# Running sums of pair units from products of two tokens' alphas, one mask operation for both score banks, and a new order

## The chip, the cores and the metric

The kernel runs on one core of one Trainium2 chip. Its metric is the device time of one execution in microseconds: 162.4 us is the median of three runs (162.36 to 163.71). A time in the text below that has a start and an end is counted from the first instruction of the profiled execution.

Five engines take part. TensorE multiplies matrices and writes PSUM, which has eight banks. VectorE, ScalarE and GpSimd work element by element[...]. SyncE (SP) issues the loads and stores, and ScalarE's queue issues a few DMA transposes. The profile calls them PE (and PEld for its weight loads), DVE, ACT, POOL and SP.

## What is computed

For 4 batches and 8 heads, 768 tokens and 48 columns a head, a gated linear recurrence runs over the tokens, and its result goes through a low-rank mixing over the tokens and a two-layer MLP:

```python
for t in range(S):
    state = alpha[:, :, t, :, None] * state + einsum('bhd,bhe->bhde', k[:, :, t], v[:, :, t])
    y[:, :, t] = einsum('bhd,bhde->bhe', q[:, :, t], state)
# x: y with the heads side by side, [4, 768, 384]
h = x.transpose(0, 2, 1) @ U @ V            # U is 768 x 32, V is 32 x 768
u = x + h.transpose(0, 2, 1)
out = u + maximum(u @ w_ch1, 0) @ w_ch2     # 384 -> 1536 -> 384
```

All inputs and the output are fp32; the matmuls run on bf16 operands.

## The kernel before

**Chunks.** The recurrence is computed in chunks. Inside a chunk, the logarithms of the alphas are summed up along the tokens by a matmul with a triangle of ones; the exponentials of the sums (`aa`) and of their negatives (`ai`) scale q and k (`rq`, `rk`); the scaled q and k are transposed (`qT`, `kT`), multiplied to scores, masked to the causal half (`pm`), and multiplied with v (`rv`). A state `st` carries the chunk's end to the next one. Its factor `tot` comes from the sums over the whole chunk.

**Two kinds of units.** Each batch has six units, u0 to u5. In batches 2 and 3 (`stage_gla`) a unit is 128 tokens of all eight heads. In batches 0 and 1 (`PAIR`, function `stage_pair`) a unit is 256 tokens of four heads: a partition holds two neighbouring tokens, 64 partitions make one chunk of 128 tokens, and a unit has two chunks one above the other. So a pair unit's `lt`, the logarithms, has two halves of 192 columns, for the first (j = 0) and the second (j = 1) token of each pair. The running sum up to the first token of a pair is the sum of all pairs before it and its own first token; up to the second token it is the sum of all pairs up to it. In the old form the sum is made of three matmuls: the triangle `upto` with the first half, written to both halves of the output (384 columns), `below` (without the pair itself) with the second half onto the first 192 columns, and `upto` with the second half onto the other 192. Four small matmuls with `onesel` make the totals, two for each half.

**Scores.** The score matmul of every unit writes two PSUM banks of 128x512, one for the even and one for the odd heads. A VectorE operation for each bank multiplies it with the mask, `maskp` in a pair unit (L542) and `maskc` in the others (L769), and writes half of `pm` in bf16.

**Mixing and MLP.** After its six units a batch goes through the mixing (`stage_mix`, to `uT`, the transposed input of the MLP), then `mlp1` (24 groups of three matmuls of 384 columns at L953, a group named here by half of the tokens and by its 128 rows of w1, each followed by a relu on ScalarE or VectorE, L963 and L965), then `mlp2` (L983, 18 groups of four or five matmuls, an addition on VectorE at L995, a store). For batch 3, `rq` and `rk` are transposed by DMA (issued on ScalarE's queue, L734), for the other batches by TensorE.

**The order.** Every step is put in a list by `P.add` with the engines that it may run on, what it reads and what it writes. The string `TABLE` is the order in which the steps are issued: a number is the step's place in the list, and a letter after it its engine where there is a choice (A ScalarE, V VectorE, G GpSimd). It was found by a search over a cost model, the class `Plan`. Each engine takes its steps in the order of the table. The costs and latencies in `P.add` and `Plan` decide only which buffer or PSUM bank of several a step is given and how many filler matmuls run before 28 us on idle TensorE; they hold nothing back on the chip. A step waits on the chip for the steps that it depends on, and for buffers that come free. `port=True` marks steps that share a port of VectorE and GpSimd.

**Loads.** Every load is one DMA of 192 KB on SP's queue into one of 36 buffers, in the order of the table; the weights come through the same buffers and are cast to bf16. SP's loads and stores and the DMA transposes share the same DMA engines.

Of the kernel before, what the change touches and what calls it, by code (L numbers as in the profile page):

```python
# [159 lines left out]
75 2 3 4 5 209 211 67 76 163 165 79 234 214 167 69 77 68 170V 212 215G 236 217 172 238 213 216V 166 169V 218 171 174V 220V 173V 175 176 83 70 81 237  # L160
168 219A 71 78 164G 80 178 221 179 223 73 72 87 74 0 241G 180 222 181 84 186 259 239 188 210G 240G 190 189 261 224 225 226 177 264 263 192V 1 193G 187G
242 227 243 244A 262 245V 229 230 231 194 246 232V 282 191 196A 233V 228 247 248 182 195 284 197A 184A 201 198 183 85 287 285 265G 82 88 202 266V 267
203 269A 235G 89 268 199 204 200 86 270A 185A 286 249 250 251 271 90 91 7 288G 254 289V 8 260G 95 6 33 99 252 256 35 31 23 39 10 290 258A 253 272 273
292A 19 41 21 37 27 25 107 29 291 255 205 274 275 293A 276 294 257A 295 296 283A 277 57 297 298 279 206 9G 410 34G 32G 412 278 299 208A 207V 300 301
302 304V 101 92 100 47 96 97 94 415 280A 281A 303A 13 16 305 306 93 43 55 45 49 14A 311 308 314 317 307A 51 63 59 53 456 315 309 433 98 103 312 17V
313A 458 318 320 310V 323 321 324 322V 325V 435 11 20V 319V 36A 316A 340 338 342 362 339V 61 436 461 438 341A 366 22G 42G 364 24A 460 363A 12A 38V 40V
365V 352 328 437 367A 414 30A 459 65 102 111 108 104 109 105 329V 343V 26V 28V 463V 106 462G 326 348 349A 506 413 330 368 354 360 355V 331V 336 508
353V 416V 439V 112 346 332 511 347A 369A 333A 372 373V 334 335V 337V 327V 440G 358 356 465 344 464 467V 510 361A 509 359A 442 411G 417G 115 113 444V
345A 357A 466A 418 441 350 419 425 443V 420V 421V 351A 46A 48A 468 15 44G 56G 50G 110 114 426 469 445 422 370 116 424 423 446 470 371A 52A 380 386 54G
64G 429 430 432V 447 58A 431A 434A 374 375 448 452 62G 427 428V 449 60V 66V 450 387 381 453 454A 117 481 483 376 457V 455V 476 471 477 382 486 485 529  # L170
484 531 377 472 512G 514 388 473V 487V 513V 474 516V 515 392 489 488V 451G 383 532 533 517A 491V 479V 389 482G 490 478 492A 480A 535G 534 653 393 496
497 493 518 498G 536G 495 494 119 394 655 537 398 538 379 378 123 390 127 399 499 520 395 519 475G 500G 530G 507A 539A 656 659V 501 521 544 540A 658
657 541 660G 503 661 545 400 502 662A 505A 522 504A 663 542 543 524 547 523G 546V 664V 526 672 549 551A 548 525 550A 674 118 391 124 121 120 129 131
528V 135 133 122 125 527V 665 552 404 676 677 553A 675 692 712 554 654G 401 666 137 139 667 132 126 564 559 555 560 556 561 405 406 557 670 562 668 565
566 694 714 567 563V 669 558A 587 585 589 696 716 695 715 717 590A 732 671V 679V 568V 573 609 605 407 610V 698G 579 615 606V 616V 571 580A 586A 588A
752 591 734 592A 697 700 577 678V 572V 701V 754 673G 719G 699G 756 737 755 680 607 134 613 608V 578V 595 575 682 687 574V 681V 688 614V 611 576A 736
612A 596A 603 702 581 601 703V 689G 597 569 599 604A 582A 735 598A 570A 863 600A 602A 683V 128 385 136 384 408 758G 739G 693G 738G 704 684 705 685 686
583 707 617 740 722 584A 708 723V 718G 865 618 690 867 130 141 403 706 159 151 147 138 757G 709V 691V 866 741A 713G 619 710 761 762A 720 742 593 759
760A 594A 721V 629 620 143 409 146 396 621 622 402 868 727 743V 630 728 140 148 145 155 724 744 898 952 916 753A 733G 18 870G 729G 763 711V 765 726 764
635 636 745 725 746 631 623 747 637 900 901 624 730 750 748 749V 766 767V 632 880 731A 882 902 751A 883 903 885 884 872 625 869G 638 626 768 628 871  # L180
641 642 152 153 627 149 397 142 769V 780 775 776 770 777 771 781 782 643 918 919 772 887G 904G 647 954 648 778 783 649 773 889 920 779V 784V 144 634
150 811 922G 923G 934 956 955 812A 921 924 774V 829 813 873 787 830V 814V 160 874 799 800V 875 650 819 793 815 794V 644 816V 936 809 827 825 810V 823
791 828V 785 905G 881G 864G 886G 899G 788A 925 907 876 906 888 957G 824V 826V 786V 877 797 803 893 821 878 157 792A 798A 938 894 804V 156 154 161 805
806V 801 158 941V 802V 937 879A 939 822A 820A 817 926 890 908 940G 818A 928 959 789 790A 892 891 909 917G 895G 958G 853 910 795 796V 943 942 807 808V
896 831 911 912 833 854 935G 960 914 947 929 927 913V 930 931V 948 949V 915A 832A 858 834 835 859 633 162 855 953V 836 837 944 946 961 945 860 838 839
950 932 652 963 962 646 964 651 645 856 843 840 861 951V 933A 965A 897A 966 848 967A 841 978 968 973 980 975 974 979 844 849 970 969 845 976 977A 857
842 862 981 850 971 982V 1015 1016V 1025 1007 1011 1013 1027 972V 991 1008V 993 994A 1028A 1026A 851 846 1009 995 1001 999 1023 1002A 1014A 1024A 992A
1021 1019 1029 1022V 1012V 1017 1010A 1020A 1018A 983 1046 1047 1030V 1048 1049 984A 989 990V 987 1051 1005 1003 1004V 639 1050 985 1052 997 1053 986V
988V 1054 640 1055 852 996A 1031 1041 1036 998V 1042 1006A 1000A 1043 1044 1032 1037 1038 1033 1056 1045 847 1039 1040 1034 1057 1059 1060 1035 1058
1061  # L190
# [8 lines left out]
def kernel(  # L199
# [37 lines left out]
    QUAD = ()  # L237
    TRD = {(3, c): "kq" for c in range(NC)}
# [78 lines left out]
    pms = Pool(slots("pm", 3, [C, HP, 2, C], BF16))  # L317
# [13 lines left out]
    P.warm = lambda: nc.tensor.matmul(ps[:, 7, :], lhsT=filler[:, 0:128], rhs=filler, start=True, stop=True)  # L331

# [96 lines left out]
    def stage_pair(b, u, sprev, xb):  # L429
# [10 lines left out]
        lt = Buf(lts)  # L440
        P.add({"ACT": 435}, lambda e: nc.scalar.activation(jh(lt()[:, :, 0:D]), raw(at), AF.Ln), r=[at], w=[lt])  # L441
# [17 lines left out]
        def f_cum(e):  # L459
            l2 = jh(lt()[:, :, 0:D])  # L460
            nc.tensor.matmul(cb()[:, 0:DM].rearrange("p (i h d) -> p i h d", i=2, d=D), lhsT=upto, rhs=l2[:, 0:1].to_broadcast([C, 2, HP, D]), start=True, stop=False)
            nc.tensor.matmul(cb()[:, 0:Q], lhsT=below, rhs=l2[:, 1], start=False, stop=False)
            nc.tensor.matmul(cb()[:, Q : 2 * Q], lhsT=upto, rhs=l2[:, 1], start=False, stop=False)
            nb = 2 if b == 0 else 1
            if b == 0:
                nc.tensor.matmul(cb()[:, DM : DM + 8], lhsT=ident, rhs=offd.rearrange("p a b -> p (a b)"), start=False, stop=False)
            tot4 = cb()[:, DM : DM + 4 * nb].rearrange("p (c a b) -> p c a b", c=2, a=2)
            for a in range(2):
                for j in range(2):
                    nc.tensor.matmul(  # L470
                        tot4[:, :, a, :], lhsT=lt()[:, HP * j + 2 * a : HP * j + 2 * a + 2, :].rearrange("t h w -> t (h w)"),
                        rhs=onesel[:, :, 0:nb], start=False, stop=(a == 1 and j == 1),
                    )

        P.add({"PE": mm(DM, Q, Q, 4, 4, 4, 4, *([8] if b == 0 else []))}, f_cum, r=[lt], w=[cb])
# [48 lines left out]
        def f_sc(e):  # L524
            for n in range(4):
                a, j = n // 2, n % 2
                for par in range(2):
                    o = 64 * par
                    for c in range(2):
                        r = slice(64 * c, 64 * c + 64)  # L530
                        nc.tensor.matmul(  # L531
                            sc[par]()[r, n * C : (n + 1) * C],
# [6 lines left out]
        def f_mask(par):  # L539
            s2 = sc[par]().rearrange("p (a j c) -> p a j c", a=2, j=2)  # L540
            dst = pm()[:, :, par, :].rearrange("p (a j) c -> p a j c", j=2)
            nc.vector.tensor_tensor(dst, s2, maskp.to_broadcast([C, 2, 2, C]), op=ALU.mult)  # L542

        for par in range(2):
            P.add({"DVE": 605}, lambda e, par=par: f_mask(par), r=[sc[par]], w=[(pm, par)])
# [63 lines left out]
        if apart:  # L609
            yb = [Buf(bank) for _ in range(2)]  # L610
            def f_yn(e):
                for h in range(HP):
                    for j in range(2):
                        for c in range(2):
                            r = slice(64 * c, 64 * c + 64)
                            for m in parts:
                                nc.tensor.matmul(
                                    yb[c]()[m, h * D : (h + 1) * D], lhsT=pm()[r, (h // 2) * 2 + j, h % 2, m], rhs=raw(rv)[r, j, h, :],
# [3 lines left out]
            P.add({"PE": mm(*[D] * 8)}, f_yn, r=[(rv, 0), (rv, 1), (pm, 0), (pm, 1)], w=[(yb[0], 0), (yb[1], 0)], mode=tile)  # L622
# [22 lines left out]
        def f_y(e):  # L645
# [12 lines left out]
            for h in range(HP):  # L658
                for j in range(2):
                    nc.tensor.matmul(  # L660
                        y[:, :, h, :], lhsT=pm()[:, (h // 2) * 2 + j, h % 2, :], rhs=rv()[:, j, h, :, :],
                        start=False, stop=(h == HP - 1 and j == 1), skip_group_check=True,
                    )
# [400 lines left out]
```

## Time and profile before

| | us |
|---|---|
| median of three runs | 162.4 |
| the profiled execution's own time | 164.51 |
| its span, first to last instruction | 162.7 |
| TensorE busy | 153.9 |
| VectorE busy | 119.3 |
| ScalarE busy | 85.4 |
| GpSimd busy | 52.8 |
| first MLP matmul starts at | 28.06 |
| first MLP matmul of batch 2 starts at | 101.67 |
| last addition of VectorE starts at | 159.79 |

A row of a timeline reads: start, length, engine, line, operation, what it writes and reads, shape, count; in brackets the idle time of the engine before it, and what ended that. A row of a table by stretches reads: from and to, length, and for each of PE, PEld, DVE, ACT and POOL the busy time with the number of instructions; then TensorE's granted clock, the busy share of the DMA engines and GB/s. In the page's slices each digit is a tenth of busy time in one fortieth of the span. Matmuls overlap: one of 384 columns is listed with 320 ns and more, but they follow each other every 0.16 us. The DMA engines are busy for nearly the whole time up to 120 us.

### The profile page before, as it was taken

What the parts mean: (1) busy time and instruction counts of PE and PEld (TensorE: products, weight loads), DVE (VectorE), ACT (ScalarE), POOL (GpSimd) and SP (SyncE); (2) the same over time, 40 slices, a digit from 0 to 9 for tenths busy, and PEclk for the clock granted to TensorE, in tenths of its full rate; (3) what the DMA queues carried; (4) which work ended last, traced back from release to release, by engine and by line L of the source; (5) the groups of instructions that cost most, each with busy time, mean ns of one, the idle gap of its engine ahead of it and who ended that gap; (6) DMA issues with size and microseconds to landing.
All of it is one profiled execution on the core that took longest, in us unless ns stands there. A gap on an engine that the chain in (4) does not pass through costs nothing.

```text
span 162.7 us, 4734 instructions
## 1 busy us (share of the span) xinstructions
PE 153.9 (95%) x1821; PEld 99.6 (61%) x1821; DVE 119.3 (73%) x275; ACT 85.4 (52%) x224; POOL 52.8 (32%) x85
## 2 busy tenths in 40 slices
PE   6899999999999999999999999896899999999992
PEld 2457677566666665766676657463576747666662
DVE  6289995788997999977487969696698777234441
ACT  5748788958836678676954661601701311472000
POOL 5256741217336460215975005533370000000000
PEclk9999999999999999999999999999999999999999
DMA  5999999998999967979988879999994631002223
GB/s 128 288 299 272 270 234 290 286 310 254 297 320 258 241 144 162 194 155 213 201 194 162 201 141 210 192 156 180 223 246 15 186 106 28 0 0 76 97 109 133
DMA packets 89910, 30.39 MB, mean 187 GB/s; under 512 B 83584, under 2 KB 89856, under 8 KB 89888
## 3 DMA queue, kind: packets, MB, share of 16 engines
q1 hardware_dynamic: 83360, 28.52, 73.9%
q10 hardware_dynamic: 6528, 1.57, 6.7%
q8 instruction: 14, 0.23, 0.6%
q14 instruction: 8, 0.07, 0.1%
HBM read 23.79 MB, written 4.72 MB: 175 GB/s over the span
## 4 chain that ended last, share of the span: by engine, by line
PE 67%; SPq 15%; DMA 12%; issue 2%; ACT 1%; DVE 1%; POOL 0%; ACTq 0%; DVEq 0%; POOLq 0%
PE ps L983 27%; PE ps L953 23%; SPq L411 10%; DMA io<-in_moe_w_ch_dram 4%; DMA io<-in_v_dram 4%; DMA qt<-rq 3%; DMA io<-in_q_dram 2%; PE ps L759 2%; PE ps L507 2%; PE ps L743 2%; SPq L387 2%; SPq L1009 2%; PE ps L926 1%; PE ps L851 1%; PE ps L531 1%
## 5 line engine op out<-in xcount | busy, mean ns | idle before, releaser
L983 PE MATMUL ps<-w_sb,h1t 128*128 128x384 bf16 (+2 forms) x300 | 53.5, 320 | 0.0
L953 PE MATMUL ps<-uT,w_sb 128*128 128x384 bf16 x288 | 51.0, 326 | 1.3 <-ACT h1t L963 0.9
L953 PEld LDWEIGHTS <-w_sb 128*128 128x128 bf16 x288 | 27.1, 98 | 17.8 <-issue 1.5
L983 PEld LDWEIGHTS <-h1t 128*128 128x128 bf16 x300 | 26.7, 98 | 16.0 <-issue 1.8
L963 ACT ACTIVATE h1t<-ps 128x384 bf16<-128x384 f32 x52 | 23.6, 497 | 20.7 <-PE ps L953 12.7
L965 DVE TENSOR_SCALAR h1t<-ps 128x384 bf16<-128x384 f32 x44 | 22.7, 552 | 11.1 <-PE ps L953 11.0
L769 DVE TENSOR_TENSOR pm<-ps,maskc 128x512 bf16<-128x512 f32 x24 | 15.1, 683 | 3.3 <-PE ps L759 3.3
L995 DVE TENSOR_TENSOR ou<-ub,ps 128x384 f32<-128x384 bf16 (+2 forms) x19 | 9.9, 528 | 9.2 <-PE ps L983 7.8
L542 DVE TENSOR_TENSOR pm<-ps,maskp 128x512 bf16<-128x512 f32 x24 | 15.6, 683 | 0.5 <-PE ps L531 0.5
L722 POOL TENSOR_TENSOR rk<-io,ai 128x384 bf16<-128x384 f32 x10 | 9.2, 923 | 19.1 <-DMA io<-in_k_dram 13.9
L342 POOL CAST rv<-io 128x384 bf16<-128x384 f32 x18 | 9.4, 527 | 16.5 <-DMA io<-in_v_dram 16.1
L338 ACT CAST xb<-ps 128x192 bf16<-128x192 f32 (+1 forms) x22 | 7.7, 377 | 12.7 <-PE ps L851 6.1
L492 POOL TENSOR_TENSOR rk<-io,ai 128x384 bf16<-128x384 f32 x7 | 6.8, 965 | 11.6 <-DMA io<-in_k_dram 7.3
L722 POOL TENSOR_TENSOR rq<-io,aa 128x384 bf16<-128x384 f32 x10 | 9.1, 914 | 4.2 <-DMA io<-in_q_dram 3.1
L911 DVE TENSOR_TENSOR ub<-xb,ps 128x384 bf16<-128x384 bf16 x18 | 8.6, 549 | 1.8 <-PE ps L903 1.8
L695 ACT ACTIVATE ai<-ps 128x384 bf16<-128x384 f32 x12 | 5.8, 498 | 4.9 <-PE ps L685 3.5
L441 ACT ACTIVATE lt<-io 128x384 bf16<-128x384 f32 x12 | 6.1, 524 | 3.6 <-DMA io<-in_alpha_dram 3.6
L342 POOL CAST w_sb<-io 128x384 bf16<-128x384 f32 x10 | 4.9, 509 | 9.4 <-DMA io<-in_moe_w_ch_dram 9.4
L696 ACT ACTIVATE aa<-ps 128x384 bf16<-128x384 f32 x12 | 5.8, 496 | 3.6 <-POOL rk L722 2.1
L338 ACT COPY kt<-ps 128x512 bf16<-128x512 bf16 x10 | 5.9, 587 | 3.0 <-PE ps L743 1.3
L492 DVE TENSOR_TENSOR rq<-io,aa 128x384 bf16<-128x384 f32 x7 | 4.5, 649 | 3.9 <-ACT aa L478 3.3
L676 ACT ACTIVATE lt<-io 128x384 bf16<-128x384 f32 x12 | 6.1, 522 | 2.0 <-DMA io<-in_alpha_dram 2.0
(133 smaller groups left out, 242.8 us busy)
## 6 DMA issues: line engine op xcount, KB each, us to landing
io<-in_alpha_dram SPq DMA_DIRECT2D x24, 192.0 KB, 4.1
io<-in_k_dram SPq DMA_DIRECT2D x24, 192.0 KB, 4.1
io<-in_q_dram SPq DMA_DIRECT2D x24, 192.0 KB, 4.2
io<-in_v_dram SPq DMA_DIRECT2D x24, 192.0 KB, 4.1
io<-in_moe_w_ch_dram SPq DMA_DIRECT2D x24, 192.0 KB, 4.1
out_dram<-ou SPq DMA_DIRECT2D x24, 96.0 KB, 3.2
out_dram<-ou SPq DMA_DIRECT2D x11, 192.0 KB, 1.9
out_dram<-ou SPq DMA_DIRECT2D x1, 128.0 KB, 1.7
```

Source lines behind the costliest of these rows:

```text
L338: nc.scalar.copy(dst, src)
L342: nc.gpsimd.tensor_copy(dst, src)
L411: lambda e: nc.sync.dma_start(t().rearrange("p (h j) d -> p h (j d)", j=2), src[b, hs, sl, :].rearrange("h (p j) d -> p h (j d)", j=2)),
L492: eng.tensor_tensor(jh(dst()[:, :, 0:D]), raw(a), jh(x()), op=ALU.mult)
L542: nc.vector.tensor_tensor(dst, s2, maskp.to_broadcast([C, 2, 2, C]), op=ALU.mult)
L722: eng.tensor_tensor(dst()[:, :, 0:D], a(), x(), op=ALU.mult)
L769: nc.vector.tensor_tensor(pm()[:, :, par, :], s2, maskc.to_broadcast([C, HP, C]), op=ALU.mult)
L953: nc.tensor.matmul(hb()[:, 0:TW], lhsT=w1_sb[:, ct, jt * 128 : (jt + 1) * 128], rhs=uT()[:, ct, tt * TW : (tt + 1) * TW], start=(ct == 0), ...
L963: nc.scalar.activation(dst, hb()[:, 0:TW], AF.Relu)
L965: nc.vector.tensor_scalar_max(dst, hb()[:, 0:TW], 0.0)
L983: nc.tensor.matmul(hb()[:, 0 : hi - lo], lhsT=h1()[:, jt, c * C : (c + 1) * C], rhs=w2_sb[:, jt, lo:hi], start=(jt == 0), stop=(jt == NJ - ...
L995: nc.vector.tensor_tensor(ou()[:, lo:hi], base()[:, c, lo:hi], hb()[:, 0 : hi - lo], op=ALU.add)
```

## The change

Four things differ.

1. In a pair unit a new step multiplies the second token's alphas by the first's, in place in the load buffer, in fp32, 128x192, on VectorE or GpSimd. The logarithm, taken after it, then holds the first token's value in its first half and the pair's sum in its second. The running sums become three matmuls of 192 columns each (`below` with the pairs, the identity with the first tokens, `upto` with the pairs), and two small matmuls make the totals.
2. One VectorE operation masks both score banks, over a view of the two PSUM banks, 128x1024 elements. `pm` is laid out with the parity ahead of the head, and its readers follow.
3. The stores of the pair batches may cover part of a row. They cover the whole row as before, since only batch 3 splits its last output.
4. The table is new. It has 1050 steps in place of 1062: 24 masks are gone and 12 products are there.

The core of the diff, without the table and without the other readers of `pm`:

```diff
+    PROD = (0, 1)
...
-    pms = Pool(slots("pm", 3, [C, HP, 2, C], BF16))
+    pms = Pool(slots("pm", 3, [C, 2, HP, C], BF16))
...
+    def two(x):
+        i, j = sorted(t.idx for t in x)
+        return ps[:, i : j + 1 : j - i, :]
+
+    def one(x, par):
+        return ps[:, sorted(t.idx for t in x)[par], :]
...
+        prod = b in PROD
+
+        def f_prod(e):
+            eng = nc.gpsimd if e == "POOL" else nc.vector
+            eng.tensor_tensor(raw(at)[:, 1], raw(at)[:, 0], raw(at)[:, 1], op=ALU.mult)
+
+        if prod:
+            P.add({"DVE": 240, "POOL": 470}, f_prod, r=[at], w=[at], port=True)
         P.add({"ACT": 435}, lambda e: nc.scalar.activation(jh(lt()[:, :, 0:D]), raw(at), AF.Ln), r=[at], w=[lt])
...
+            if prod:
+                nc.tensor.matmul(cb()[:, 0:Q], lhsT=below, rhs=l2[:, 1], start=True, stop=False)
+                nc.tensor.matmul(cb()[:, 0:Q], lhsT=ident, rhs=l2[:, 0], start=False, stop=False)
+                nc.tensor.matmul(cb()[:, Q : 2 * Q], lhsT=upto, rhs=l2[:, 1], start=False, stop=False)
+            else:
+                nc.tensor.matmul(cb()[:, 0:DM].rearrange("p (i h d) -> p i h d", i=2, d=D), lhsT=upto, rhs=l2[:, 0:1].to_broadcast([C, 2, HP, D]), start=True, stop=False)
+                nc.tensor.matmul(cb()[:, 0:Q], lhsT=below, rhs=l2[:, 1], start=False, stop=False)
+                nc.tensor.matmul(cb()[:, Q : 2 * Q], lhsT=upto, rhs=l2[:, 1], start=False, stop=False)
...
-                for j in range(2):
+                for j in range(1 if prod else 0, 2):
...
-        def f_mask(par):
-            s2 = sc[par]().rearrange("p (a j c) -> p a j c", a=2, j=2)
-            dst = pm()[:, :, par, :].rearrange("p (a j) c -> p a j c", j=2)
-            nc.vector.tensor_tensor(dst, s2, maskp.to_broadcast([C, 2, 2, C]), op=ALU.mult)
-
-        for par in range(2):
-            P.add({"DVE": 605}, lambda e, par=par: f_mask(par), r=[sc[par]], w=[(pm, par)])
+        def f_mask(e):
+            s2 = two(sc).rearrange("p r (a x) -> p r a x", a=2)
+            m2 = maskp.rearrange("p o j c -> p o (j c)").unsqueeze(1).to_broadcast([C, 2, 2, 2 * C])
+            nc.vector.tensor_tensor(pm().rearrange("p r (a j) c -> p r a (j c)", j=2), s2, m2, op=ALU.mult)
+
+        P.add({"DVE": 1140}, f_mask, r=[sc[0], sc[1]], w=[pm])
...
-        for par in range(2):
-            P.add({"DVE": 605}, lambda e, par=par: f_mask(par), r=[sc[par], "maskc"], w=[(pm, par)])
+        def f_mask(e):
+            s2 = two(sc).rearrange("p r (hp c) -> p r hp c", c=C)
+            nc.vector.tensor_tensor(pm(), s2, maskc.unsqueeze(1).to_broadcast([C, 2, HP, C]), op=ALU.mult)
+
+        P.add({"DVE": 1140}, f_mask, r=[sc[0], sc[1], "maskc"], w=[pm])
```

What the two tables say of the steps that the text below uses, with the numbers turned into names (b1u2 is unit 2 of batch 1; cum the running sums; m1 a group of the first MLP layer, by half and rows; rv, d, sc, y the cast of v, the state's matmul, the scores and the output; X the DMA transposes; w1.g a cast of w1's quarter g):

```
products, new: VectorE  b0u4 b0u0 b0u1 b0u3 b0u5 b1u0 b1u3, GpSimd  b0u2 b1u1 b1u2 b1u4 b1u5
SP, old:   b0u2.a b0u0.a ... (16th) b0u5.a ... (24th) b0u5.v ... (30th) w1.2 b1u2.a w1.2 w1.2 (33rd)
SP, new:   b0u0.a b0u2.a b0u4.a ... (19th) b0u5.a ... (26th) b0u4.v ... (30th) w1.1 w1.0 w1.0 w1.0 (33rd) ... (45th) w1.2
TensorE, old, before the MLP:  b1u2.cum ... b1u1.cum, m1 0.7 ...   new:  b1u1.cum, m1 0.0 ...
VectorE, old:  uT00 uT11 uT12 w1.0 uT10 relu ...
VectorE, new:  uT00 uT10 w1.1 relu w1.1 w1.3 relu b1u0.rq b1u3.product w1.2 relu relu relu ...
SP, batch 3, old:  ... b3u0.k u2.k u1.q u4.a [store] u3.k u3.q [store] u2.q [store] u0.v u1.k [store] u2.v u5.k u4.q u4.k u3.v ...
SP, batch 3, new:  ... b3u0.q u0.k u0.v u1.a u1.q [store] u3.q u2.k u3.k [store] u1.k u1.v u5.q u2.q u4.a u5.k u3.v ...
GpSimd, batch 3, old:  u0.rq ... u0.rk u1.rq u2.rk u3.rk u3.rq u2.rq u1.rv u0.rv u1.rk u2.rv ...
GpSimd, batch 3, new:  u0.rk [one copy for the mixing] u3.rq u0.rv u2.rk u1.rq u1.rv u1.rk u3.rk u2.rq u5.rk u3.rv ...
ScalarE, new:  b3u0.Xq ... u0.Xk ... u3.Xq relu relu u1.Xq relu u1.Xk u5.ai u3.Xk relu u4.ln u2.Xk u2.Xq relu ...
TensorE, MLP of batch 2, old:  three m1, b3u0.sc, five m1, u4.cum, six m1, u0.d, two m1, u1.d, ...
TensorE, MLP of batch 2, new:  two m1, b3u0.d, five m1, u0.sc, two m1, u1.d, three m1, u0.y, ...
```

## The prediction

> **What bounds the kernel now.** I read the page's busy time and its 40 slices first, then the busy time by stretch, then TensorE's timeline at the two places where the stretches have holes.
>
> ```profile
> span 162.7 us, 4734 instructions
> ...
> PE 153.9 (95%) x1821; PEld 99.6 (61%) x1821; DVE 119.3 (73%) x275; ACT 85.4 (52%) x224; POOL 52.8 (32%) x85
> ...
> PE   6899999999999999999999999896899999999992
> ```
>
> TensorE is busy 95% of the span. The slices dip at the start (where 5.9 us are filler matmuls, so TensorE is busier there than it is useful) and once more two thirds through. The stretches say how much:
>
> ```profile
> 24.00:28.06 4.06, 4.06 (x55) 2.90 (x52) 2.07 (x5) 3.68 (x11) 0.51 (x1) 1.00 0.94 288
> 28.06:30.04 1.98, 1.62 (x13) 0.88 (x10) 1.43 (x5) 1.89 (x8) 0.00 (x0) 1.00 0.82 268
> 30.04:100.00 69.96, 69.94 (x887) 46.13 (x887) 59.31 (x128) 46.79 (x124) 28.63 (x43) 1.00 0.94 218
> 100.00:120.00 20.00, 17.23 (x167) 10.91 (x165) 15.23 (x30) 6.85 (x20) 10.33 (x14) 1.00 1.24 194
> ```
>
> The first pair in a row is length and TensorE's busy time. From 30.04 to 100 it is idle 0.02 us of 70: there only less TensorE work helps. It is idle 0.36 us between 28.06 and 30.04 and 2.77 us between 100 and 120. Before 28.06 (the first MLP matmul) the chain of batch 0 sets the pace: in 10 to 25 us VectorE is busy 13.6 of 15 us. What follows is TensorE's timeline around 27 us, then its four waits after 100 us.
>
> ```profile
> 26.30 0.33 PE L461 MATMUL ps<-lt,blocks 128*128 128x384 bf16 x1
> 26.46 0.25 PE L462 MATMUL ps<-lt,blocks 128*128 128x192 bf16 x1
> 26.54 0.25 PE L463 MATMUL ps<-lt,blocks 128*128 128x192 bf16 x1
> 26.62 0.24 PE L470 MATMUL ps<-onesel,lt 128*128 128x2 bf16 x4
> 26.73 0.32 PE L891 MATMUL ps<-vp_sb,utx 128*128 128x384 bf16 x1
> ...
> 30.04 1.14 PE L953 MATMUL ps<-uT,w_sb 128*128 128x384 bf16 x6 [0.36 <-DVE uT L340]
> ```
>
> ```profile
> 103.89 0.40 PE L759 MATMUL ps<-qt,kt 48*128 48x128 bf16 x8 [0.60 <-ACT ai L695]
> ...
> 111.87 0.34 PE L782 MATMUL ps<-rv,rk 128*128 128x96 bf16 x4 [0.67 <-POOL rk L722]
> ...
> 113.76 1.62 PE L953 MATMUL ps<-uT,w_sb 128*128 128x384 bf16 x9 [0.86 <-ACT h1t L963]
> ...
> 116.31 0.62 PE L759 MATMUL ps<-qt,kt 48*128 48x128 bf16 x16 [0.60 <-ACT h1t L963]
> ```
>
> The four sum to 2.73 us. They have one root: rk of unit b3u1 ran on GpSimd at 110.90, after 2.30 us of waiting for its k. The ScalarE queue, which issues the DMA transposes in order, had its next relu at 113.22 after 7.47 us without one, so TensorE had no free bank.
>
> **What the Trainium skill says.** "VectorE: DVE Perf Modes", What auto-detection actually checks: a two-source op gets at most the two-per-cycle mode, and only where all is 16-bit; the mask (fp32 scores) and the product (fp32 alphas) therefore take one element a cycle. The trace agrees: 512 columns took 681 to 683 ns and 192 took 352, so 1.03 ns an element and some 150 ns fixed. "SBUF — State Buffer", SBUF: two separate sides: a VectorE op with two SBUF inputs and a GpSimd op lock each other out. The trace fits: rq on VectorE took 559 ns at the median and once 1135. "TensorE: Matmul & The Clock Gate", Back-to-back issue gap: columns/2.4 + 2.5 ns. The trace agrees (0.16 us from L461 to L462, 0.08 for 192 columns).
>
> **The change, part by part.** All is summed against the profiled execution: 164.51 us, a span of 162.72 and 1.79 around it. The median of the runs is 162.4, so I scale by 162.4/164.51 = 0.987 at the end.
>
> **Running sums.** Before: 26.30 to 26.73, 0.43 us a unit. After: three matmuls of 192 columns at 0.08 and two of the four small ones (0.11 for four): 0.24 + 0.055 = 0.295, saving 0.135. For the six units of batch 0 the work lies inside the stretch that TensorE does not set: nothing. In batch 1, u0 stays in that stretch; u2 and u1 stood between the mixing and the first MLP matmul. The new order leaves only u1 there: -0.43 - 0.135 = -0.565. What could eat this is the copy of uT02, which ended at 27.77; ScalarE now does one Ln and no weight cast ahead of it, so I count the gain. After 28 us: u2 comes in (+0.295), u3, u4, u5 get shorter (-0.405): -0.11.
>
> **Products.** Twelve operations of 128x192 fp32, seven on VectorE at 0.35 (the 352 ns row), five on GpSimd at 0.51 (its 128x192 row, 508 ns). GpSimd's, and VectorE's one in batch 1, lie under a busy TensorE. Six on VectorE fall in the batch-0 chain (five of batch 0, and b1u0): 2.1 us. Each Ln also waits for its product: the first rq moves from 6.72 us to some 7.8. **Masks.** 1024 elements cost 0.15 + 1.07 = 1.22 against 1.37: 0.15 saved each, 3.6 us of VectorE in all, of which 0.9 in batch 0. Nothing reads half of pm before, so the joint operation delays no reader; the first score bank comes free some 0.5 us later, which I put at 0 (-0.1 to +0.4).
>
> Batch 0 as a whole: VectorE's list up to the last xb sums to 18.2 us before (12 masks, 10 st, 6 scalings, 4 transposed copies, 4 xb) and 18.4 after (6 masks at 1.22, 6 products, 10 st, 5 scalings, 3 copies, 3 xb, one rv). Four products use VectorE's idle time ahead of the first rq. But SP now issues u5's alpha as its 19th load, not 16th, and the last v as 26th, not 24th; u5's scalings end near 20.5 us, and six state scalings, copies and masks (4.6 us) follow in a row. I take +0.6 for the end of batch 0, between -0.2 and +1.3.
>
> **The new order elsewhere.** VectorE now copies uT10 directly after uT00 and casts weights later; the wait of 0.36 goes (-0.36), and no weight is next in line, since the first MLP groups' weights are complete with the 33rd issue, as before. Between 30 and 100 us the old order had no hole; a new one can only have more. VectorE waits there for q and alpha loads and the cast of w1.2.0 (45th load; the load in that place was issued at 29.70 and takes about 4.3) with three relus behind it: +0.4, from 0 to 1.5. The stores of pair batches cover the same whole rows: 0.
>
> **Batch 3.** The loads of b3u0's q, k, v and u1's alpha, q now go out together, and u1's k ahead of u5's and u4's. By position in the SP queue and old issue times, u3's q lands near 101, u1's k at 105 and v at 106. GpSimd does u0.rk, u3.rq, u0.rv, u2.rk, u1.rq, u1.rv, u1.rk (0.91 and 0.51 each): u0.rv ready near 102.5, u1.rk near 107.4. TensorE has b3u0's d third in the MLP of batch 2 (it began at 101.67), waiting some 0.4, and b3u1's d after seven more groups of 0.49, waiting 1.1; I add 0.2 for banks. 1.7 in place of 2.73: -1.0, between -2.7 and +2.5.
>
> **Sum:** +0.6 - 0.565 - 0.11 - 0.36 + 0.4 - 1.0 = -1.04. 164.51 - 1.04 = 163.47, times 0.987 is 161.4 us.
>
> **Rivals.** (1) *The order fits and all holes close*: the first part costs nothing, no new hole, batch 3 without waits: -0.565 - 0.11 - 0.36 - 2.73 = -3.77, 160.74, scaled 158.7. For it: VectorE loses 1.2 us net; against: the first Ln is later by its product, and transposes still need ScalarE. (2) *GpSimd's queue stops batch 3*, slower. u3.rq stands in front of u0.rv, and u3's q is issued behind a store that waits for VectorE. If that q lands 3 us later (104), u0's d waits 3.3, u1.rk comes at 110.4 and u1's d waits 0.6 more. On VectorE sm of u1 stands ahead of the relus, on ScalarE the transposes do: 1.3 for banks. 5.2 against 2.73 is +2.47; with the rest (-0.04) 166.9, scaled 164.8. It decides from 4.4 us of waiting there (1% worse). For it: GpSimd waited 13.9 us for k loads on this line before. (3) *VectorE and the loads set the start, and the work saved is idle time*: batch 0 at +1.3, holes at +1: 164.8, scaled 162.7; it lies inside the no-change band, and I count it with the main case.
>
> **How the numbers follow.** 1% (1.6 us) is about what a measurement of this kernel can tell from no change. Main case 0.54, 160.2 to 162.9, of which 0.14 lies under 160.8; rival 1 0.20; rival 2 0.26. Faster 0.34, same 0.40, slower 0.26. The range 159.2 to 165.0 leaves out about half of rival 1 and under half of rival 2; it takes in both ends of the batch-0 and hole terms.
>
> **What would show it.** Matmuls of the running sums: 36 of 192 columns, 24 small totals in the pair units, 0.29 us a unit. Masks: 24 of 128x1024 at 1.22 us. Products at 0.35 and 0.51. First MLP matmul between 27.6 and 28.8 us, no wait for uT after it. Waits on TensorE in the MLP of batch 2 near 1.7 us, at d of b3u0 and b3u1. VectorE about 118 us busy. Wrong if the mask over two banks runs well off 1.2 us, if holes over 1 us stand between 30 and 100, or if TensorE waits over 4 us in batch 3.

## The result, and the profile after

The changed kernel takes 199.8 us, the median of four runs (197.3 to 200.8), beside 162.4 for the kernel before in the same comparison. The ratio is 1.223 (95% interval 1.209 to 1.236). The forecast was 161.4 us in a range of 159.2 to 165.0. It was wrong by 38 us, and no rival came near.

This is the page of the changed kernel, its totals and two rows of the 40 slices. The profiled execution is the longest of the four, 200.8 us:

```profile
span 199.0 us, 4680 instructions
...
PE 165.3 (83%) x1798; PEld 104.6 (53%) x1800; DVE 118.2 (59%) x254; ACT 87.2 (44%) x228; POOL 56.7 (28%) x90
...
PE   7586477999929976779999768999698967999993
...
PEclk9999955699987995766999996999999999999999
```

VectorE has 118.2 us of work, as forecast (about 118). TensorE has 23 matmuls less on record than before and yet 11 us more busy time, and it is idle for 33.7 us where it was idle for 8.8. The slices show where: holes up to the 34th slice, and a clock well below full speed in ten of the slices in and behind the holes. The stretch from 30 to 100 us, in which TensorE had been idle for 0.02 us, reads so after the change (length and TensorE's busy time first, its clock in the third place from the end):

```profile
30.00:100.00 70.00, 58.93 (x670) 37.16 (x670) 41.13 (x85) 34.96 (x96) 20.88 (x33) 0.82 0.76 185
```

Eleven us of holes, and a clock of 0.82. What TensorE waited for is in its list of waits (in total, how many times, longest; L562 is the mask of the pair units, L788 that of the others):

```profile
PE ps L1001 <- DVE pm L562: 6.9, 3, 3.6
PE ps L636 <- DVE pm L562: 4.4, 4, 1.4
...
PE ps L477 <- DVE pm L562: 2.0, 1, 2.0
PE ps L704 <- DVE pm L788: 1.8, 1, 1.8
...
PE ps L1001 <- DVE pm L788: 1.5, 2, 0.8
PE ps L921 <- DVE pm L788: 1.4, 1, 1.4
PE ps L867 <- DVE pm L788: 1.4, 1, 1.4
PE ps L762 <- DVE pm L788: 1.4, 1, 1.4
PE ps L527 <- DVE pm L562: 1.3, 1, 1.3
...
PE ps L869 <- DVE pm L788: 1.1, 1, 1.1
```

These sum to 23.2 us of waiting for a mask, in 16 waits. The same list of the kernel before has none. The odd thing is on the left. Only L636 and L869 read `pm` (5.5 us). L1001 is the second MLP layer, L477 and L704 are running sums, L527 transposes, L921 is the mixing, L867 the product of q with the state, L762 transposes: none of them reads what the mask writes.

A step that doesn't read `pm` may still have to wait for a mask, when it writes one of the two score banks that the mask reads. The order's placement tells the bank of every step, so each wait can be sorted. Four waits, 5.1 us, are of that kind (L477, L921, L867 and one of 0.2 us at L636). Two, 2.5 us, are of steps that read this mask's `pm`. The other ten, 15.6 us, are of steps that neither read this mask's `pm` nor write its banks: they write banks that lie between the two. Two of the waits at L636 are among these; they read the `pm` of another unit.

The groups of the masks give their number, busy time and mean length, and behind the last bar VectorE's idle time ahead of them with what ended most of it. The length is as forecast, 1.22 us. New is the idle time: 25.6 us in all, ended by transposes (L762), MLP matmuls (L1001) and others. Before, in the two rows below them, it was 3.8 us for all 48 masks, and ended by the score matmuls alone (L531 and L759).

```profile
L562 DVE TENSOR_TENSOR pm<-ps,maskp 128x1024 bf16<-128x1024 f32 x12 | 14.5, 1223 | 14.1 <-PE ps L762 2.7
L788 DVE TENSOR_TENSOR pm<-ps,maskc 128x1024 bf16<-128x1024 f32 x12 | 14.4, 1222 | 11.5 <-PE ps L1001 5.2
```

```profile
L542 DVE TENSOR_TENSOR pm<-ps,maskp 128x512 bf16<-128x512 f32 x24 | 15.6, 683 | 0.5 <-PE ps L531 0.5
L769 DVE TENSOR_TENSOR pm<-ps,maskc 128x512 bf16<-128x512 f32 x24 | 15.1, 683 | 3.3 <-PE ps L759 3.3
```

One instance, from the timeline of the changed kernel, shows what happens (start, length, engine, line, what it writes and reads; in brackets the idle time of the engine and what ended it):

```profile
16.39 0.39 PE L527 MATMUL ps<-ident,rk 128*128 128x128 bf16 x4
...
16.89 1.22 DVE L562 TENSOR_TENSOR pm<-ps,maskp 128x1024 bf16<-128x1024 f32 x1 [0.69 <-PE ps L527]
...
18.14 0.59 ACT L345 COPY kt<-ps 128x512 bf16<-128x512 bf16 x1 [2.01 <-DVE pm L562]
18.16 0.38 PE L527 MATMUL ps<-ident,rq 128*128 128x128 bf16 x4 [1.30 <-DVE pm L562]
```

The mask is that of unit b0u3, and the order's placement gave its scores the banks 2 and 6. The transposes of `rk` ahead of it belong to another unit and write bank 3, those of `rq` behind it write bank 4, and the copy on ScalarE reads bank 3. The mask waits for the first transposes, and the copy and the second transposes wait for the mask, although it touches none of these banks. They lie *between* its two. The view that the mask reads is `ps[:, i : j + 1 : j - i, :]`: two banks out of the stretch from i to j, by a step.

### The profile page after: what moved, and what is told of

Read it like the earlier page. It is cut to its first block, busy times and chain, and to the rows that moved or that the text cites. A ratio compares the mean times of both kernels' runs of the same rounds, so it can differ in the third digit from the quotient of the medians.

```text
span 199.0 us, 4680 instructions
## 1 busy us (share of the span) xinstructions
PE 165.3 (83%) x1798; PEld 104.6 (53%) x1800; DVE 118.2 (59%) x254; ACT 87.2 (44%) x228; POOL 56.7 (28%) x90
## 4 chain that ended last, share of the span: by engine, by line
PE 72%; DVE 14%; DMA 4%; ACT 4%; issue 2%; SPq 1%; POOL 1%; DVEq 0%; ACTq 0%
PE ps L1001 25%; PE ps L971 23%; DVE pm L562 7%; DVE pm L788 7%; PE ps L527 2%; DMA io<-in_alpha_dram 2%; PE ps L636 2%; DMA qt<-rq 2%; PE ps L778 2%; PE ps L762 2%; PE ps L944 2%; SPq L418 1%; PE ps L648 1%; PE ps L551 1%; PE ps L887 1%
## 5 line engine op out<-in xcount | busy, mean ns | idle before, releaser
L1001 PE MATMUL ps<-w_sb,h1t 128*128 128x384 bf16 (+2 forms) x300 | 59.7, 343 | 8.4 <-DVE pm L562 6.9
L1001 PEld LDWEIGHTS <-h1t 128*128 128x128 bf16 x300 | 28.2, 103 | 27.9 <-issue 15.7
L983 DVE TENSOR_SCALAR h1t<-ps 128x384 bf16<-128x384 f32 x49 | 25.2, 551 | 13.0 <-PE ps L971 12.7
L981 ACT ACTIVATE h1t<-ps 128x384 bf16<-128x384 f32 x47 | 22.2, 505 | 23.2 <-PE ps L971 19.4
L562 DVE TENSOR_TENSOR pm<-ps,maskp 128x1024 bf16<-128x1024 f32 x12 | 14.5, 1223 | 14.1 <-PE ps L762 2.7
L788 DVE TENSOR_TENSOR pm<-ps,maskc 128x1024 bf16<-128x1024 f32 x12 | 14.4, 1222 | 11.5 <-PE ps L1001 5.2
L741 POOL TENSOR_TENSOR rq<-io,aa 128x384 bf16<-128x384 f32 x8 | 7.3, 911 | 24.5 <-ACT aa L715 16.2
L512 POOL TENSOR_TENSOR rq<-io,aa 128x384 bf16<-128x384 f32 x8 | 7.4, 926 | 14.3 <-DMA io<-in_v_dram 10.8
L811 POOL TENSOR_TENSOR st<-sm,tot 128x384 bf16<-128x384 f32 x6 | 5.0, 829 | 22.1 <-DVE sm L823 22.1
L636 PE MATMUL ps<-rv,pm 64*128 64x48 bf16 x192 | 5.2, 194 | 4.4 <-DVE pm L562 4.4
L349 POOL CAST w_sb<-io 128x384 bf16<-128x384 f32 x15 | 7.3, 504 | 4.1 <-DMA io<-in_moe_w_ch_dram 4.1
```

Source lines behind the costliest of these rows:

```text
L512: eng.tensor_tensor(jh(dst()[:, :, 0:D]), raw(a), jh(x()), op=ALU.mult)
L562: nc.vector.tensor_tensor(pm().rearrange("p r (a j) c -> p r a (j c)", j=2), s2, m2, op=ALU.mult)
L636: nc.tensor.matmul(yb[c]()[m, h * D : (h + 1) * D], lhsT=pm()[r, h % 2, (h // 2) * 2 + j, m], rhs=raw(rv)[r, j, h, :], start=(h == 0 and j ...
L741: eng.tensor_tensor(dst()[:, :, 0:D], a(), x(), op=ALU.mult)
L788: nc.vector.tensor_tensor(pm(), s2, maskc.unsqueeze(1).to_broadcast([C, 2, HP, C]), op=ALU.mult)
L981: nc.scalar.activation(dst, hb()[:, 0:TW], AF.Relu)
```

## The theories

**Theory S, the stretch.** The waits take a view over banks i and j for the whole stretch from i to j. So the mask must wait for all that was queued on the banks between, and the later users of those banks wait for the mask. Of the 24 units only b0u2 (banks 4 and 5) and b0u0 (0 and 1) have neighbouring score banks in the changed kernel; the other 22 have one to six banks between, 2.7 on average over all 24.

**Its rivals.** A joint mask holds both banks until its end and makes the readers of the first half wait for the second. Or reading over two banks is what is slow, whatever lies between. Or the new order is at fault: it moves the loads, the engines and the steps of batch 3. Or the products, which put a step ahead of each logarithm.

## The experiments

**The joint operation taken apart.** In the changed kernel, the step of the mask issues two operations of 128x512, one a bank, in the same place; all else stays (the like at L788).

```diff
-            s2 = two(sc).rearrange("p r (a x) -> p r a x", a=2)
-            m2 = maskp.rearrange("p o j c -> p o (j c)").unsqueeze(1).to_broadcast([C, 2, 2, 2 * C])
-            nc.vector.tensor_tensor(pm().rearrange("p r (a j) c -> p r a (j c)", j=2), s2, m2, op=ALU.mult)
+            for par in range(2):
+                s2 = one(sc, par).rearrange("p (a j c) -> p a j c", a=2, j=2)
+                dst = pm()[:, par].rearrange("p (a j) c -> p a j c", j=2)
+                nc.vector.tensor_tensor(dst, s2, maskp.to_broadcast([C, 2, 2, C]), op=ALU.mult)
```

> The changed kernel, its order, banks and products as they are; only the mask step issues two VectorE operations of 128x512, one for each bank, in place of one of 128x1024 over both. Theory S (span): the view over two banks is waited for as if it touched every bank between them, so the mask waits for strangers and strangers for it; then this kernel has no wait of TensorE for a mask outside yn and y, and takes 160 to 164 us. Rival O (order): the new order itself stalls; then it stays at 195 to 200. Rival P (products ahead of the logarithms): also 195 to 200.

Measured: 162.87 us, ratio to the kernel before 1.0024 (0.9997 to 1.0051). Nearly all of the loss is the joint operation. Its page:

```profile
span 160.8 us, 4727 instructions
...
PE 152.6 (95%) x1798; PEld 99.2 (62%) x1800; DVE 119.6 (74%) x278; ACT 86.9 (54%) x228; POOL 57.9 (36%) x90
...
PE   7968889999999999999999999999999999999992
...
PEclk9999999999999999999999999999999999999999
```

TensorE now waits for a mask for 0.6 us in all. L637 reads `pm`, L590 is the state's matmul:

```profile
PE ps L637 <- DVE pm L563: 0.4, 2, 0.2
...
PE ps L590 <- DVE pm L563: 0.2, 1, 0.2
```

Between this span and the changed kernel's lie 38.2 us, and they are two things: 25.5 us of TensorE's idle time (33.7 against 8.2) and 12.7 us of busy time for the same 1798 instructions (165.3 against 152.6), which ran at a mean clock of 0.913 in place of 1.000. The Trainium skill's page "TensorE: Matmul & The Clock Gate", Part 1: The HAM clock gate, says that the array is throttled to half speed after a window of idleness and comes back with activity. The rows above fit: in the changed kernel the clock's digit falls to 5, half, right after two slices in which TensorE was busy for 6 and 4 tenths (15 to 25 us), and to 7 after the one with 2; in the kernel with two mask operations, whose longest wait is 1.2 us, the clock stays full. How much idleness it takes isn't read from slices: the second one, with 5 tenths, and some later ones with 6 leave the clock at 9. So the waits cost half as much again through the clock.

**The new order alone.** In the kernel just described, the products are left out as well and the running sums are the old ones; what is left of the change is the order.

```diff
-            eng = nc.gpsimd if e == "POOL" else nc.vector
-            eng.tensor_tensor(raw(at)[:, 1], raw(at)[:, 0], raw(at)[:, 1], op=ALU.mult)
+            pass
...
-            if prod:
+            if False:
...
-                for j in range(1 if prod else 0, 2):
+                for j in range(2):
```

> The new order with two masks of 128x512 in each mask step and without the products; the running sums are the old five to eight matmuls. The step of the product is empty. S expects 160 to 164 us, within 1 us of the kernel with products. O expects 195 to 200. P expects 161 to 164 here, and 195 to 200 for the kernel with products and split masks.

Measured: 162.72 us, ratio 1.0009 (0.9983 to 1.0036). The order costs nothing and brings nothing. With products and shorter sums it was 162.87, so these bring nothing either that the runs can tell from none.

**The joint operation alone.** The kernel before, its order and sums kept; the first mask of a unit does both banks, the second is left empty, and `pm` is laid out as in the change.

```diff
+            turns.append(par)
+            if len(turns) > 1:
+                return
+            s2 = two(sc).rearrange("p r (a x) -> p r a x", a=2)
...
+            nc.vector.tensor_tensor(pm().rearrange("p r (a j) c -> p r a (j c)", j=2), s2, m2, op=ALU.mult)
```

> The kernel before, its order and banks, with only the two masks of a unit replaced by one joint operation at the place of the first. The two banks have 1.6 banks between them on average (changed kernel: 2.7). S expects it much slower than 162.4, 175 to 195 us, and less slow than the changed kernel. O and P expect 161 to 164.

Measured: 189.3 us at the median of four runs that reach from 186.0 to 193.5, without an interval; even the lowest is 23.7 us above the 162.3 of the kernel before. The loss doesn't need the new order. The old placement leaves 1.6 banks between on average, and the loss is smaller than in the changed kernel, as theory S expects. But not all of it is the stretch: with neighbouring banks this order still loses some 7 us (below, under "Without the new order").

**The two banks side by side.** In the changed kernel, the placement chooses for a score pair the two free banks with the least distance; the joint mask stays. 22 of the 24 units then have neighbours, and two in batch 3 have gaps of one and two banks.

```diff
+                _, at, i, j = min(
+                    (j - i, max(free[i], free[j]), i, j) for i in range(8) for j in range(i + 1, 8) if not held[i] and not held[j]
+                )
```

> The changed kernel with one mask operation of 128x1024 as it is, but the plan gives the two score banks next to each other in 22 of 24 units (a gap of one and of two banks in the other two). S expects 160 to 166 us and masks at 1.22 us. A rival J, that one operation over two banks is itself what hurts (its length, or both banks held until its end), expects 185 to 200. Rivals O and P expect 195 to 200.

Measured: 164.78 us, ratio 1.0122 (1.0054 to 1.0190). The same number of joint masks, the same hold of both banks, the same readers, and 35 of the 37 us are gone. The two groups of masks of this kernel:

```profile
L803 DVE TENSOR_TENSOR pm<-ps,maskc 128x1024 bf16<-128x1024 f32 x12 | 14.3, 1219 | 2.3 <-PE ps L793 2.2
L577 DVE TENSOR_TENSOR pm<-ps,maskp 128x1024 bf16<-128x1024 f32 x12 | 14.3, 1216 | 1.4 <-PE ps L566 1.4
```

One takes as long as over distant banks (1219 and 1216 ns against 1222 and 1223), so the reading is no slower over a distance; and it waits almost only for its own score matmuls (L793, L566). This rules out the joint hold and the two-bank reading as the main cause, and leaves the stretch.

**The two banks far apart.** The same edit with `i - j` for `j - i` takes the two free banks with the greatest distance, 4.3 banks between on average. It was run with the joint mask and, as its twin, with two operations.

> The same banks with one joint mask of 128x1024. S expects more than the changed kernel's 199.8 us, since 4.3 banks lie between against 2.7: 205 to 235, with the clock of TensorE granted lower still. B expects the time of the kernel with the same banks and two masks.

> The changed kernel with the score banks placed as far apart as the plan has them free (4.3 banks between them on average) and two masks of 128x512. Theory S (the span of the joint view is what waits) expects no effect of the distance as long as each bank has its own operation: 161 to 166 us. A rival B, that the placing of the banks itself makes the waits, expects over 180.

Measured: 207.7 us with the joint mask (two runs, 206.7 and 208.8), ratio 1.278 (1.267 to 1.289), the slowest of all; with two operations on the very same banks the ratio is 1.0102 (1.0020 to 1.0184). The placing costs 1%, the joint mask across the gaps some 26%. TensorE's list of waits for the joint one has the same kinds of steps as the changed kernel's, which don't read `pm` (L1016 and L719 are the second MLP layer and running sums here):

```profile
PE ps L1016 <- DVE pm L577: 5.0, 2, 3.6
...
PE ps L1016 <- DVE pm L803: 3.8, 2, 2.5
PE ps L719 <- DVE pm L803: 3.6, 1, 3.6
```

**Three gaps and no other.** In the changed kernel, the three units with six banks between (b1u4, b1u5, b2u1) keep the joint mask, the other 21 have two operations.

```diff
+            if abs(sc[0].idx - sc[1].idx) == 7:
...
+            else:
+                for par in range(2):
```

> The changed kernel with split masks in 21 units and the joint mask in three: b1u4, b1u5 and b2u1, the units whose score banks have six banks between them. S prices a unit with strangers between its banks at (199.8 - 162.9) / 22 = 1.7 us on average, more with more banks between: 167 to 173 us. If the loss were a single place in the changed kernel elsewhere, it takes 162.9.

Measured: 169.72 us, ratio 1.0431 (1.0356 to 1.0507), where all in two operations had 1.0024. Three masks cost (1.0431 - 1.0024) x 162.4 = 6.6 us, 2.2 us each on average. The waits for them on TensorE are one a unit:

```profile
PE ps L1015 <- DVE pm L566: 1.9, 1, 1.9
...
PE ps L645 <- DVE pm L566: 1.4, 1, 1.4
PE ps L771 <- DVE pm L798: 1.4, 1, 1.4
```

By the placement the waiting steps write banks 3, 5 and 6, and 3 (L645 reads the `pm` of another unit), all between the mask's 0 and 7.

**What is left with neighbours.** Three kernels on the neighbouring banks: the joint mask in the 22 neighbours and two operations in the two gaps; the same, but no joint mask in batch 0; and two operations everywhere. The edit of the first is below; the second has `and b > 0` behind the condition, the third no condition and two operations.

```diff
-            s2 = two(sc).rearrange("p r (a x) -> p r a x", a=2)
...
+            if abs(sc[0].idx - sc[1].idx) == 1:
...
+            else:
+                for par in range(2):
```

> Neighbouring banks with the joint mask in 22 units, and two operations of 128x512 in the two units whose banks have others between them (both in batch 3). If those two gaps make what the kernel with neighbouring banks lost to the one with split masks (164.8 against 162.9), this takes 162.5 to 163.3. If the rest is that the joint mask holds the first bank and the first half of pm until its end, above all in batch 0, it stays at 164 to 165.

> As with neighbouring banks and the joint mask in 22 units, but two masks in the six units of batch 0. If the joint mask costs in the batch-0 chain, which VectorE sets, this takes 162.5 to 163.3; if only the placing of the banks costs, 163.6 to 164.2.

> The changed kernel with neighbouring score banks (22 of 24) and two masks of 128x512 everywhere. It splits what the joint mask on neighbouring banks lost to split masks on the plan's own banks (163.8 against 162.9): if the placing of the banks lost it, this takes 163.5 to 164.2; if the joint mask's longer hold did, 162.5 to 163.2.

Measured: 163.84 (ratio 1.0096, 1.0072 to 1.0120), 163.95 (1.0086, 1.0058 to 1.0113) and 164.04 (1.0106, 1.0055 to 1.0157). These three can't be told apart: in this order the joint mask over neighbours neither costs nor brings anything that the runs can tell. What the two gaps had cost can't be told either: 1.0122 with a joint mask there and 1.0096 without lie inside each other's intervals. That all three are 1% above the kernel before is the price of the placement, which takes banks for their place and not for being free first: with two operations, it is the ratio of 1.0106 against 1.0024.

**Without the new order.** Two kernels have the parts in the old order. In the first, the old order and sums, neighbouring banks where there were any (21 units), the joint mask there and two operations in the other three.

```diff
+            if abs(sc[0].idx - sc[1].idx) > 1:
...
+                nc.vector.tensor_tensor(dst, s2, maskp.to_broadcast([C, 2, 2, C]), op=ALU.mult)
+                return
+            if len(turns) >= 2:
+                return
```

> The kernel before, its order and running sums, with neighbouring score banks in 21 units and one joint mask there at the place of the first; the other three keep two masks. S expects that nothing is left of the 189.3 us that the joint mask cost in this order with the plan's own banks: 161.5 to 165. If a joint mask in the old order was slow because it comes at the place of the first one, 170 to 190.

Measured: 169.91 us, ratio 1.0430 (1.0379 to 1.0481), a miss. TensorE is idle for 1.5 us between 30 and 60 us and waits for masks in several places, most of them steps that don't read `pm` (L792 is the score matmul of another unit, L1026 the second MLP layer):

```profile
PE ps L792 <- DVE pm L812: 1.4, 1, 1.4
...
PE ps L603 <- DVE pm L575: 0.9, 3, 0.5
...
PE ps L1026 <- DVE pm L575: 0.7, 2, 0.4
```

No bank lies between a joint mask's two here, so by theory S these waits must be for the mask's own banks. By the placement they are: all nine waits for a mask in this execution, 4.5 us, are of steps that write one of that mask's two banks (L792, for one, writes bank 5 behind a mask over 4 and 5). The placement moved these banks, and the joint step, at the place of the first mask, holds them for longer. This order with neighbouring banks and two masks was not run, so which of the two costs how much was not separated, and stays open. The joint mask over neighbours is thus shown to be free in the new order only.

In the second, the old order again, with products and short sums in batch 1 alone. A product is issued on VectorE directly ahead of its logarithm.

```diff
+        def f_ln(e):
+            if b == 1:
+                nc.vector.tensor_tensor(raw(at)[:, 1], raw(at)[:, 0], raw(at)[:, 1], op=ALU.mult)
+            nc.scalar.activation(jh(lt()[:, :, 0:D]), raw(at), AF.Ln)
```

> The kernel before, its order, banks and split masks, with the product and the shorter sums in batch 1 only; the product runs on VectorE just ahead of its logarithm. The sums save 0.135 us of TensorE six times, 0.8 us, of which five fall in or just ahead of the full stretch: I expect 161.4 to 162.2 where the kernel before takes 162.3. If TensorE's saved time only turns into a wait for the loads of batch 3, it takes 162.3 as before.

Measured: 168.1 us at the median of six runs that reach from 164.3 to 171.1, with no interval; a miss as well, though with this spread its size isn't known. The list of waits of the profiled execution, one of 168.3 us, points to a reason:

```profile
ACT lt L445 <- DVE io L444: 6.2, 3, 3.4
...
PE ps L468 <- ACT lt L445: 2.1, 2, 1.6
```

The product takes some 0.37 us, but it stands in VectorE's queue where the logarithm stood in ScalarE's, behind work that VectorE still has to do. Three logarithms waited 6.2 us for it, and TensorE 2.1 us for two of them. That a product's price is its place in a queue fits this; since the lowest run is only 1.9 us above the kernel before, it is argued and not shown. In the new order the products cost nothing that the runs can tell.

No kernel here beats the kernel before.

## Why the prediction was wrong

**The step that failed** is the one on the masks: "Nothing reads half of pm before, so the joint operation delays no reader; the first score bank comes free some 0.5 us later, which I put at 0 (-0.1 to +0.4)". It asked who reads what the operation writes, and how long its own two banks are held. It didn't ask what the view covers. The view with its step was in the diff, and the placement of the banks could be worked out from the plan. The term came to +37 us: in the changed kernel 23.2 us of TensorE's waits for a mask, 15.6 of them for banks between, and 12.7 us of slower clock behind them (38.2 us of span in all). None of the rivals had this mechanism. The list of what would prove it wrong had its sign, though: the 11 us of holes between 30 and 100 us. Its other sign, a mask well off 1.2 us, did not appear: the operation took 1.22 us and was no dearer for its distance.

**The other steps** can be read from the kernel with two mask operations, in which the failed term is absent. It takes 162.87 us, inside the range. That is in part luck: the start lost more than was put down and batch 3 gained more, and the two errors offset each other. Here are its stretches, cut where the prediction cut them:

```profile
28.06:30.04 1.98, 1.98 (x19) 1.38 (x18) 1.29 (x3) 1.69 (x5) 1.04 (x2) 1.00 1.07 353
30.04:100.00 69.96, 69.76 (x887) 46.29 (x885) 57.32 (x123) 49.14 (x131) 29.54 (x43) 1.00 0.91 215
100.00:120.00 20.00, 19.63 (x189) 12.72 (x188) 17.99 (x37) 7.58 (x22) 10.37 (x14) 1.00 1.27 211
```

| step | predicted | measured |
|---|---|---|
| end of batch 0 (start of its mixing, 24.70 before) | +0.6 (-0.2 to +1.3) | 26.39: +1.7 |
| from there to the first MLP matmul (3.36 before) | -0.565 | 2.73: -0.63 |
| running sums of one unit | 0.295 us | 0.30 |
| wait for uT behind the first MLP matmuls | -0.36 | gone |
| new holes from 30 to 100 us | +0.4 (0 to 1.5) | 0.20 |
| idle from 100 to 120 us (2.77 before) | -1.0 (-2.7 to +2.5) | 0.37: -2.4 |
| a product on VectorE, on GpSimd | 0.35, 0.51 us | 0.36, 0.59 |

- **Batch 0** was sized too low, and out of its own range. The order alone, without products, had this mixing at 26.22, so 1.5 of the 1.7 us are the order and only 0.17 the products. The prediction named the later load of b0u5 as the reason, and put the end of this unit's scalings near 20.5; they ended at 21.84. How much of that is the load and how much VectorE's queue was not separated. So the first MLP matmul came at 29.12 in place of about 28.1.
- **Running sums** were right, within 0.07 us before the MLP and to the hundredth in a unit. From the timeline of this kernel, one unit's sums from 28.82 to the first MLP matmul at 29.12:

```profile
28.82 0.25 PE L477 MATMUL ps<-lt,blocks 128*128 128x192 bf16 x1
28.90 0.25 PE L478 MATMUL ps<-lt,ident 128*128 128x192 bf16 x1
28.98 0.25 PE L479 MATMUL ps<-lt,blocks 128*128 128x192 bf16 x1
29.07 0.19 PE L490 MATMUL ps<-onesel,lt 128*128 128x2 bf16 x2
29.12 0.48 PE L973 MATMUL ps<-uT,w_sb 128*128 128x384 bf16 x2
```

- **Batch 3** was right in sign and gained more than twice what was put down; rival 2, GpSimd's queue, doesn't show: one wait of 0.37 us for a transpose is all that is left there. The waits that the prediction put at the `d` of b3u0 and b3u1, 0.4 and 1.1 us, don't appear, so the size came out of no step that it had right. It had also read the four holes of the kernel before wrongly: they can't have one root at 110.90, since the first of them had ended at 103.89, on `ai`.
- **The scaling at the end** hid a part of the error. The profiled execution of before took 164.51 us, 1.3% above its median, and the prediction put that share on everything alike. The span of the kernel with two mask operations is 1.9 us shorter than that execution's, but its median is the same as before's (162.87 and 162.29 in that comparison), and its own profiled execution (162.54) lies near its median. So what is gained between two profiles is not gained between the medians, and some of the holes priced, those in batch 3 likely, may have belonged to that one execution. No second profile of the kernel before was taken to tell; this is argued, not shown.

On the waits around PSUM the prediction cited no page. One bears on it: the Trainium skill's "PSUM — Partial Sum Buffer", PSUM bank collisions raise a hardware error, says that semaphores must guard PSUM by bank and quadrant. Whoever takes that for all that is guarded would expect an access to banks 2 and 6 to have nothing to do with 3 and 4. The guards in these kernels are coarser, as the 1.30 us wait on bank 4 at 18.16 shows, and the measurement decides.

## What to carry to other kernels

Before you join two operations into one, write down the address range of the joint view, first byte to last, and ask who uses anything within it, not only who uses its elements; if strangers do, put the parts side by side or leave two operations. The price of an operation that an engine waits for is not its duration alone but what it locks: joining saved 0.14 us a unit of VectorE's time and cost 1.5 us a unit, 36.9 us over 24. And when TensorE's busy time grows with the same instructions, look at its clock, then for the waits in front of it.

## What the runs showed of the hardware

- A VectorE operation read two PSUM banks at the same rate at every distance that was run: 1024 columns took 1216 and 1219 ns where 22 of 24 pairs were neighbours, 1222 and 1223 where 22 of 24 had banks between, against 2 x 680 ns in two operations. The saving of 0.14 us for a unit was nowhere to be seen in the time.
- Such an operation over banks i and j was ordered, in these kernels, against uses of the banks between, in both directions. In the new order it cost nothing with no bank between (ratios 1.0096 and 1.0086 with it, 1.0106 without); with six between 2.2 us a unit; with 2.7 on average 37 us in 24 units; with 4.3 on average some 43 us, (1.278 - 1.010) x 162.4. The waits stand in the instruction streams as semaphores; which layer puts them there, the runs don't tell.
- TensorE's waits of 1 to 4 us, scattered over the span, went with a mean clock of 0.913 and digits of half in places, and 8% more busy time for the same 1798 instructions; with two mask operations, without these waits, the clock was 1.000.
